# Attention with a threshold and a two-layer network: the first loads through one queue, the first row maximum ahead of a low part, the first x loaded earlier, and three instructions on the row sums on GpSimd

## The chip, the core and the metric

The kernel runs on one core of a Trainium2 chip. The metric is the time of one execution in microseconds on the device, the median of several runs. TensorE (PE) multiplies matrices, VectorE (DVE), ScalarE (ACT) and GpSimd (POOL) work on rows of 128 partitions, and SyncE (SP) issues most transfers. Each engine takes its instructions in the order of its own queue and waits for others by semaphores.

## The reference

```python
scores = (1 / sqrt(64)) * q @ k.T          # batch 8, heads 8, 576 x 576 each, head_dim 64
thresh = max(scores, row) - tau            # tau = 0.02
scores = where(scores >= thresh, scores, -1e9)
attn = exp(scores - max(scores, row))
attn = attn / (sum(attn, row) + 1e-9)
x = (attn @ v)                             # heads side by side: 4608 rows x 512
h = x @ w_in                               # 512 x 2048, float64 weights
g = maximum(h, 0) + alpha * minimum(h, 0)
out = g @ w_out                            # 2048 x 512
```

Only the few scores of a row that lie within tau of the row's maximum count. The products are made as sums of three products of a high part and a low part of each operand.

## The kernel before, in words

The 64 heads are taken as 32 pairs (class Pair), and each pair in nine units: four blocks of 128 queries for each of the two heads, and one unit "t" for the remaining 64 queries of both. The main loop runs over cycles, one for each unit. In cycle i TensorE makes the scores of unit i + 2 (`scores`, tile s: the high part of k, then the low part) and transposes the masked rows of unit i (`turn`, tile t); VectorE takes the row maximum (`rowmax`, nmx, L456) and later masks and sums (`mask`, L476: p times the comparison with thr, and the row's sum into sm); ScalarE makes the exponentials and the threshold (`expo`, L464 and L469). A score tile has two buffers, so the scores of one unit wait for the mask of the unit two before.

Everything else is put into cycles by tables: PREP (loads and the splitting of the next pair's q and k), AVW and AVS (products with v), FINW and FINS (the end of a pair: `recip`, `rturn`, `rout`, `fin_add`, `fin_mul`, `fin_out`). Within a cycle the functions are called in the order in which the tables were entered. The order on TensorE, ScalarE, VectorE and GpSimd is the order of these calls; only the queue of SyncE is ordered by a scheduler.

Pairs 0 to 4 are the whole pairs (WHOLE = 5): their masked rows are not split into high and low parts. While they run, the float64 weights of the first layer's seven chunks are decoded (class Split64) in steps on all three vector engines: `size` on ScalarE, `clamp`, `shift`, `sign` and `power` on VectorE (L143, L146, L151, L156), `rest` and `join` on GpSimd (L77; wri and wti or wro and wto are the temporaries, wi and wo the weights). GpSimd also makes the low part of the next pair's k (kl) and q (qt).

At the end of a pair `recip` makes rv = 1 / (sm + 1e-9) from nine columns of sums; for whole pairs sm + 1e-9 is first multiplied with min(sm + 1e-9, 1). TensorE turns rv (`rturn`), ScalarE copies it (`rout`), it goes to DRAM (rvd) and comes back spread over partitions (rb), and GpSimd multiplies x with it (`fin_mul`). x goes to DRAM (xs).

Pair 0 has its own loading: `load_first` issues two halves for each of two heads, q on ScalarE's queue and k on SyncE's; `prep_first` makes the high part of q (ScalarE, L359), its low part (VectorE, L360), the high part of k (L361) and its low part (L362) for one head.

Once 256 rows of x are complete, the first layer's work on them begins (class Mlp): a cycle loads them (`load_x`, tile xr, from cycle 49 on), XO0 cycles later GpSimd splits them in four parts (`split_part`, L214 and L215), and then TensorE makes one chunk of the hidden layer (tile pha, L226) in every cycle that has room. After the last pair the rest of the network runs alone.

## Time and profile before

| | before |
|---|---|
| median of 3 runs | 1360.91 us (1358.39 to 1362.42) |
| the profiled execution | 1360.37 us |
| its span, first to last instruction | 1358.6 us |
| TensorE busy | 1324.9 us (98%) |
| VectorE busy | 973.6 us (72%) |
| ScalarE busy | 842.4 us (62%) |
| GpSimd busy | 970.8 us (71%) |
| HBM read and written | 105 GB/s over the span |

The busy times are of the whole span; what a stage waits for is seen only in that stage. The lines of the profile name a line of the kernel, the engine, the operation, and the tile that is written and those that are read.

### The profile page before, as it was taken

What the parts mean: (1) busy time and instruction counts of PE and PEld (TensorE: products, weight loads), DVE (VectorE), ACT (ScalarE), POOL (GpSimd) and SP (SyncE); (2) the same over time, 40 slices, a digit from 0 to 9 for tenths busy, and PEclk for the clock granted to TensorE, in tenths of its full rate; (3) what the DMA queues carried; (4) which work ended last, traced back from release to release, by engine and by line L of the source; (5) the groups of instructions that cost most, each with busy time, mean ns of one, the idle gap of its engine ahead of it and who ended that gap; (6) DMA issues with size and microseconds to landing.
All of it is one profiled execution on the core that took longest, in us unless ns stands there. A gap on an engine that the chain in (4) does not pass through costs nothing.

```text
span 1358.6 us, 24051 instructions
## 1 busy us (share of the span) xinstructions
PE 1324.9 (98%) x8041; PEld 1162.3 (86%) x8041; DVE 973.6 (72%) x1843; ACT 842.4 (62%) x1910; POOL 970.8 (71%) x1369
## 2 busy tenths in 40 slices
PE   6988999999999999999999999999999999999999
PEld 4655799999999999999999999988888888888887
DVE  6989889889888888888888874665565744333332
ACT  7888888888888888888888873433332321211110
POOL 3766899899889898988988985775665754433431
PEclk9999999999999999999999999999999999999999
DMA  8653544644544645545445414345555443343222
GB/s 241 183 160 104 152 131 121 166 128 120 160 134 124 165 127 142 140 132 144 141 136 146 117 51 127 109 132 170 183 164 196 134 145 124 109 152 113 93 78 86
DMA packets 113595, 186.04 MB, mean 137 GB/s; under 512 B 16608, under 2 KB 47872, under 8 KB 113472
## 3 DMA queue, kind: packets, MB, share of 16 engines
q1 hardware_dynamic: 113152, 183.92, 46.2%
q8 instruction: 64, 1.05, 0.3%
q10 hardware_dynamic: 320, 0.59, 0.2%
q14 instruction: 59, 0.48, 0.1%
HBM read 104.41 MB, written 37.90 MB: 105 GB/s over the span
## 4 chain that ended last, share of the span: by engine, by line
PE 83%; DVE 6%; ACT 6%; POOL 1%; DMA 1%; issue 1%; ACTq 0%; SPq 0%; POOLq 0%; DVEq 0%
PE acca L256 12%; PE pha L226 12%; PE s L441 10%; PE phc L226 9%; PE av L620 8%; PE accc L256 8%; PE accb L256 7%; PE phb L226 7%; PE t L485 7%; DVE p L476 2%; DVE nmx L456 2%; PE tk L501 1%; PE accc L981 1%; ACT p L464 1%; ACT xh L205 1%
## 5 line engine op out<-in xcount | busy, mean ns | idle before, releaser
L456 DVE TENSOR_REDUCE nmx<-s 128x1 f32<-128x576 f32 x288 | 217.2, 754 | 67.8 <-PE s L441 65.3
L256 PE MATMUL acca<-wo,ga 128*128 128x512 f32 x756 | 224.1, 415 | 0.9 <-ACT xb L631 0.9
L476 DVE SCALAR_TENSOR_TENSOR p<-s,thr,p 128x576 f32<-128x576 f32 x256 | 206.6, 807 | 4.5 <-ACT thr L469 4.4
L464 ACT ACTIVATE p<-s,nmx 128x576 f32<-128x576 f32 x256 | 189.8, 741 | 8.7 <-DVE nmx L456 8.4
L441 PE MATMUL s<-kh,qst 128*128 128x288 f32 x640 | 141.6, 311 | 27.9 <-DVE p L476 16.2
L250 POOL TENSOR_TENSOR gc<-ptc,gc 128x512 fp32r<-128x512 f32 x45 | 58.1, 1292 | 144.0 <-ACT gc L247 144.0
L226 PE MATMUL pha<-xh,wi 128*128 128x256 f32 x784 | 157.9, 285 | 0.2 <-ACT pra L239 0.2
L485 PE MATMUL t<-ident,p 128*128 128x128 f32 x1024 | 154.5, 273 | 0.0
L247 ACT ACTIVATE gc<-ptc 128x512 fp32r<-128x512 f32 x45 | 28.4, 632 | 196.8 <-DVE ptc L951 196.8
L256 PEld LDWEIGHTS acca<-wo,ga 128*128 128x128 f32 x756 | 133.5, 190 | 19.1 <-ACT xb L631 1.4
L441 PEld LDWEIGHTS s<-kh,qst 128*128 128x128 f32 x640 | 100.1, 191 | 54.6 <-issue 26.4
L226 PEld LDWEIGHTS pha<-xh,wi 128*128 128x128 f32 x784 | 128.0, 190 | 6.5 <-ACT pra L239 3.6
L441 PE MATMUL s<-kl,qst 128*128 128x288 f32 x640 | 133.1, 298 | 0.0
L485 PEld LDWEIGHTS t<-ident,p 128*128 128x128 f32 x1024 | 124.4, 141 | 1.3 <-DVE e L551 1.0
L942 POOL TENSOR_TENSOR homexl<-homexr,homexh 128x512 fp32r<-128x512 f32 (+1 forms) x84 | 103.2, 1247 | 22.1 <-ACT homexh L941 22.0
L226 PE MATMUL phc<-homexh,wi 128*128 128x512 f32 x360 | 112.5, 389 | 0.0
L226 PE MATMUL pha<-xl,wi 128*128 128x256 f32 x392 | 110.7, 283 | 0.0
L578 POOL TENSOR_TENSOR rt<-kw,rt 64x128 fp32r<-64x128 f32 x216 | 97.8, 453 | 17.3
L256 PE MATMUL accc<-wo,gc 128*128 128x512 f32 x480 | 110.1, 389 | 0.0
L250 POOL TENSOR_TENSOR ga<-pta,ga 128x256 fp32r<-128x256 f32 x126 | 96.0, 763 | 18.5 <-ACT ga L247 10.1
L256 PEld LDWEIGHTS accc<-wo,gc 128*128 128x128 f32 x480 | 90.1, 188 | 18.7
L551 DVE TENSOR_TENSOR eo<-t,eo 128x512 fp32r<-128x512 f32 (+1 forms) x162 | 94.7, 598 | 12.7 <-ACT eo L547 11.5
(160 smaller groups left out, 3345.2 us busy)
## 6 DMA issues: line engine op xcount, KB each, us to landing
kr<-in_k_dram SPq DMA_DIRECT2D x31, 320.0 KB
rb<-rvd SPq DMA_DIRECT2D x64, 144.0 KB
xs<-xa SPq DMA_DIRECT2D x32, 288.0 KB
pinb<-part SPq DMA_DIRECT2D x36, 256.0 KB
part<-obb SPq DMA_DIRECT2D x36, 256.0 KB
pinc<-part SPq DMA_DIRECT2D x36, 256.0 KB
out_dram<-obc SPq DMA_DIRECT2D x35, 256.0 KB
qr<-in_q_dram SPq DMA_DIRECT2D x31, 288.0 KB
```

The costliest lines, as they stand in the source:

```text
L226: nc.tensor.matmul(ph[:, :n], w[:, c, :], xx[:, c, :n], start=(c == 0 and ti == 0), stop=(c == NCC - 1 and ti == 2),)
L250: nc.gpsimd.tensor_tensor(g[:, 1, :n], t[:, :n], f(g[:, 0, :n]), op=ALU.subtract)
L256: nc.tensor.matmul(acc[:m, :], gg[:, g, o : o + m], w, start=(first and ti == 0), stop=(last and ti == 2))
L441: nc.tensor.matmul(ps[:, h, :288], w, kk[:, a + h * 288 : a + (h + 1) * 288], start=(ki == 0 and i == 0), stop=(ki == 1 and i == n - 1),)
L456: nc.vector.tensor_reduce(self.nmx[:, j : j + 1], self.S[u][0][:, :, :288], axis=AX.XY, op=ALU.max, negate=True)
L464: nc.scalar.activation(pj, ps[:, :, :288], AF.Exp, bias=nmx[:, j : j + 1], scale=1.0)
L476: nc.vector.scalar_tensor_tensor(pj, ps[:, :, :288], thr[:, j : j + 1], pj, op0=ALU.is_ge, op1=ALU.mult, accum_out=self.sm[:, c : c + 1])
L485: nc.tensor.transpose(tb[:, c, :], pt[:, j, j * D + c * P : j * D + (c + 1) * P], ident)
L551: nc.vector.tensor_tensor(dst[1], ps, f(dst[0]), op=ALU.subtract)
L578: nc.gpsimd.tensor_tensor(lo, r, f(hi), op=ALU.subtract)
L620: nc.tensor.matmul(pa[:m, :n], w, x, start=(part == 0 and c == 0), stop=c == NKC)
L942: self.low.tensor_tensor(xl[:, c, :n], xr[:, c, :n], f(xh[:, c, :n]), op=ALU.subtract)
```

## The change

Five things are done together. The eight first transfers all go through SyncE's queue, q ahead of k for each head, and ScalarE's first instruction is the Exp that loads its table. On VectorE the first row maximum stands ahead of the low part of the second head's k, and the negative tau behind it. For whole pairs the sums' addition, minimum and product are three GpSimd instructions, with a new tile ru; VectorE keeps the reciprocal. The first x is split one cycle after its load in place of two, so that layer 1 begins one cycle earlier. Pair 4 has its own table FINL: its reciprocal is turned and sent later, and the load of the first x stands ahead of it.

```diff
+FINL = (9, 12, 14, 14, 18, 19)
-XO, XO0 = 1, 2
+XO, XO0 = 1, 1
...
-            for eng, r, src, e in ((nc.scalar, qr, q, 0), (nc.sync, self.kr, k, D)):
-                for j in range(2):
-                    w = S + j * e
+            for j in range(2):
+                for r, src, w in ((qr, q, S), (self.kr, k, S + j * D)):
                     for half in range(2):
-                        eng.dma_start(
+                        nc.sync.dma_start(
...
             nc.scalar.activation(self.kh[:, c], self.kr[:, c], AF.Copy)
+            if j == 0:
+                self.prep_first_kl(c)
+
+        def prep_first_kl(self, c):
             nc.vector.tensor_tensor(self.kl[:, c], self.kr[:, c], f(self.kh[:, c]), op=ALU.subtract)
...
-            nc.vector.tensor_scalar(self.rv, self.sm, 1e-9, None, op0=ALU.add)
             if self.whole:
-                nc.vector.scalar_tensor_tensor(self.rv, self.rv, 1.0, self.rv, op0=ALU.min, op1=ALU.mult)
+                ru = ap1.tile([P, 9], F32, tag="ru", name=f"ru{self.pi}", bufs=1)
+                nc.gpsimd.tensor_scalar(ru, self.sm, 1e-9, 1.0, op0=ALU.add, op1=ALU.min)
+                nc.gpsimd.tensor_scalar(self.rv, self.sm, 1e-9, None, op0=ALU.add)
+                nc.gpsimd.tensor_tensor(self.rv, self.rv, ru, op=ALU.mult)
+            else:
+                nc.vector.tensor_scalar(self.rv, self.sm, 1e-9, None, op0=ALU.add)
             nc.vector.reciprocal(self.rv, self.rv)
...
-        fin = FINW if p.whole else FINS
+        fin = (FINW, FINL)[p.pi == WHOLE - 1] if p.whole else FINS
...
+        nc.scalar.activation(ntau_sb, ident[:, :1], AF.Exp)
         p.load("k")
-        nc.scalar.activation(ntau_sb, ident[:, :1], AF.Exp)
...
-        nc.vector.tensor_scalar(ntau_sb, tau_sb, -1.0, None, op0=ALU.mult)
         p.load("v")
         for i in range(-3, total + TAIL):
             if i == -1:
+                do(0, "rowmax")
+                p.prep_first_kl(slice(S, KW))
+                nc.vector.tensor_scalar(ntau_sb, tau_sb, -1.0, None, op0=ALU.mult)
+                do(0, "expo")
...
-            else:
+            elif i > 0:
                 do(i + 1, "rowmax")
                 do(i + 1, "expo")
```

The start, on VectorE before: the low parts of q and k of both heads, the negative tau, and then the row maxima of the first two units.

```order
L360 SCALAR_TENSOR_TENSOR qst0_111<-qr0_175,qst0_111 64x576
L362 TENSOR_TENSOR kl0_194<-kr0_174,kh0_193 128x640
L1152 TENSOR_SCALAR ntau_sb_66<-tau_sb_65 128x1
L456 TENSOR_REDUCE nmx0_0_219<-s0_0_209 128x1
L456 TENSOR_REDUCE nmx0_0_219<-s0_1_214 128x1
L476 SCALAR_TENSOR_TENSOR p0_0_222,sm0_208<-s0_0_209,thr0_0_220,p0_0_222 128x576
```

The same place now, with the line numbers of the changed kernel:

```order
L360 SCALAR_TENSOR_TENSOR qst0_111<-qr0_176,qst0_111 64x576
L460 TENSOR_REDUCE nmx0_0_212<-s0_0_207 128x1
L366 TENSOR_TENSOR kl0_194<-kr0_175,kh0_193 128x640
L1165 TENSOR_SCALAR ntau_sb_66<-tau_sb_65 128x1
L460 TENSOR_REDUCE nmx0_0_212<-s0_1_220 128x1
L480 SCALAR_TENSOR_TENSOR p0_0_217,sm0_206<-s0_0_207,thr0_0_213,p0_0_217 128x576
```

The row maximum of unit 0 moved ahead of the low part of the second head's k.

The end of pair 4, on VectorE before (rv4 is made from the sums sm4; wto6 is a weight being decoded, s5_1 and s5_2 are scores of pair 5):

```order
L456 TENSOR_REDUCE nmx5_0_1603<-s5_1_1610 128x1
L636 TENSOR_SCALAR rv4_1656<-sm4_1285 128x9
L638 SCALAR_TENSOR_TENSOR rv4_1656<-rv4_1656 128x9
L639 RECIPROCAL rv4_1656<-rv4_1656 128x9
L151 SCALAR_TENSOR_TENSOR wto6_1566<-wro6_1482,wto6_1566 128x512
L456 TENSOR_REDUCE nmx5_2_1666<-s5_2_1638 128x1
```

VectorE keeps only the reciprocal there (L647 now); the instructions that it waits for stand on GpSimd now as follows, between the joining of the weight wo5 and the low part of pair 6's q:

```order
L78 TENSOR_TENSOR wro5_1354<-wro5_1354 128x256 x2
L78 TENSOR_TENSOR wto5_1460<-wto5_1460,wo5_1572 128x256 x2
L78 TENSOR_TENSOR wo5_1572<-wto5_1460,wro5_1354 128x256 x2
L642 TENSOR_SCALAR ru4_1665<-sm4_1291 128x9
L643 TENSOR_SCALAR rv4_1664<-sm4_1291 128x9
L644 TENSOR_TENSOR rv4_1664<-rv4_1664,ru4_1665 128x9
L407 TENSOR_TENSOR qt6_1698<-qr6_1634,qst0_111 128x576
```

At pairs 0 and 1 the three stand between wti and wi of a weight, at pair 2 between wi and the next wro, and at pair 3, as here, between wo and qt.

The first x, on TensorE before (pha0_0 is the first chunk of layer 1, s6_1 a unit of scores of pair 6):

```order
L691 MATMUL filler2_1905<-ident_60 128x128 x3
L441 MATMUL s6_1_1929<-kh6_1594,qst0_111 128x288 x2
L441 MATMUL s6_1_1929<-kl6_1596,qst0_111 128x288 x2
L485 MATMUL t5_8_1935<-ident_60,p5_3_1853 128x128 x4
L501 MATMUL tk5_3_1940<-ident_60,p5_3_1853 128x128
L226 MATMUL pha0_0_1949<-xh256_0_1802,wi0_358 128x256
```

Now the chunk's matmuls follow the filler at once, and s6_1 stands behind the twelve of them:

```order
L699 MATMUL filler2_1919<-ident_60 128x128 x3
L227 MATMUL pha0_0_1929<-xh256_0_1806,wi0_358 128x256
L227 MATMUL pha0_0_1929<-xl256_0_1807,wi0_358 128x256
L227 MATMUL pha0_0_1929<-xh256_0_1806,wi0_358 128x256 x2
L227 MATMUL pha0_0_1929<-xl256_0_1807,wi0_358 128x256
```

Layer 1's chunks and the sums of layer 2 on the first 256 rows each stand one cycle earlier from here until pair 9.

## Rows read from the trace of the kernel before

**Rows 1.** Busy time by stage: the stretch and its length in us, then for each engine the busy us and the number of instructions, the granted clock of TensorE, the share of the DMA engines, and GB/s.

```profile
0.00:30.00 30.00, 16.86 (x81) 14.06 (x82) 19.30 (x36) 20.63 (x42) 9.54 (x29) 0.94 0.94 272
30.00:140.00 110.00, 100.24 (x538) 65.42 (x536) 98.99 (x192) 95.31 (x209) 75.13 (x96) 1.00 0.53 147
140.00:200.00 60.00, 55.85 (x400) 49.94 (x399) 51.78 (x108) 51.03 (x122) 52.79 (x89) 1.00 0.51 137
200.00:800.00 600.00, 596.65 (x4342) 563.70 (x4341) 525.19 (x1094) 521.31 (x1247) 537.52 (x894) 1.00 0.49 134
```

**Rows 2.** Waits of TensorE from 30 to 140 us: who waited for whom, us in total, times, the longest.

```profile
PE s L441 <- DVE p L476: 9.3, 11, 2.3
```

**Rows 3.** Timeline of the start: start us, duration us, engine, line, operation, tiles, and in brackets the idle time before and who ended it.

```profile
0.73 2.49 ACTq L347 DMA_DIRECT2D qr<-in_q_dram  x4
...
0.74 2.76 SPq L347 DMA_DIRECT2D kr<-in_k_dram  x4
...
5.24 0.68 ACT L359 ACTIVATE qst<-qr 128x576 fp32r<-128x576 f32 x1 [0.49 <-DMA qr<-in_q_dram]
...
8.38 0.68 ACT L359 ACTIVATE qst<-qr 128x576 fp32r<-128x576 f32 x1 [1.28 <-DMA qr<-in_q_dram]
...
8.97 0.72 ACT L361 ACTIVATE kh<-kr 128x640 fp32r<-128x640 f32 x1
...
11.65 0.76 DVE L456 TENSOR_REDUCE nmx<-s 128x1 f32<-128x576 f32 x1 [0.22 <-PE s L441]
```

**Rows 4.** What the DMA engines moved from 0 to 20 us, in 40 slices of 0.5 us.

```profile
GB/s 0 0 0 0 235 295 281 244 181 209 260 216 235 218 167 225 346 364 378 387 406 357 375 363 358 344 346 352 342 352 354 359 363 389 410 360 360 354 366 361
```

**Rows 5.** The chain of waits from 30 to 180 us, some of its pieces: start us, us, what.

```profile
36.70 0.36 DVE rv L636
...
37.99 0.97 DVE wti L151
...
61.60 0.32 DVE rv L636
...
62.79 0.79 DVE wti L146
...
87.25 0.54 DVE rv L638
...
88.64 0.74 DVE nmx L456
...
112.10 0.47 DVE rv L636
...
114.22 1.51 DVE wto L143
...
137.65 0.36 DVE rv L636
...
138.94 0.97 DVE wto L151
...
172.35 1.49 PE pha L226 x12
```

**Rows 6.** Timeline of GpSimd at the ends of the whole pairs (columns as in Rows 3; x2 are two halves).

```profile
36.30 1.42 POOL L77 TENSOR_TENSOR wti<-wti,wi 128x256 f32<-128x256 f32 x2
...
60.47 1.41 POOL L77 TENSOR_TENSOR wti<-wti,wi 128x256 f32<-128x256 f32 x2
...
85.19 1.42 POOL L77 TENSOR_TENSOR wi<-wti,wri 128x256 fp32r<-128x256 f32 x2
...
90.01 2.01 POOL L77 TENSOR_TENSOR qt<-qr,qst 128x288 fp32r<-128x288 f32 x2 [0.70 <-ACT qr L393]
...
112.47 1.43 POOL L77 TENSOR_TENSOR wo<-wto,wro 128x256 fp32r<-128x256 f32 x2
113.87 1.58 POOL L403 TENSOR_TENSOR qt<-qr,qst 128x576 fp32r<-128x576 f32 x1
...
138.62 1.87 POOL L77 TENSOR_TENSOR wo<-wto,wro 128x256 fp32r<-128x256 f32 x2
140.65 1.41 POOL L403 TENSOR_TENSOR qt<-qr,qst 128x576 fp32r<-128x576 f32 x1 [0.15 <-ACT qr L393]
```

**Rows 7.** GpSimd's groups of instructions by line and shape: busy us and mean ns of one, idle us before.

```profile
L578 POOL TENSOR_TENSOR rt<-kw,rt 64x128 fp32r<-64x128 f32 x216 | 97.8, 453 | 17.3
...
L663 POOL TENSOR_SCALAR vs<-xa 64x1 f32<-64x1 f32 x54 | 11.1, 206 | 4.7
...
L108 POOL MEMSET eps_sb<- 128x1 f32 x1 | 0.1, 95 | 0.0
```

**Rows 8.** Timeline of VectorE, one row (columns as in Rows 3).

```profile
90.65 0.71 DVE L151 SCALAR_TENSOR_TENSOR wto<-wro,wto 128x512 int32<-128x512 int32 x1
```

**Rows 9.** TensorE's idle times in its timeline, and two windows with the granted clock (columns as in Rows 3 and Rows 1).

```profile
23.29 0.58 PE L441 MATMUL s<-kh,qst 128*128 128x288 f32 x2 [1.94 <-DVE p_t L476]
...
116.61 0.50 PE L441 MATMUL s<-kh,qst 128*128 128x288 f32 x2 [2.33 <-DVE p L476]
...
24.00:27.00 3.00, 3.00 (x16) 2.95 (x16) 2.43 (x6) 1.85 (x6) 2.83 (x5) 0.50 1.08 265
110.00:120.00 10.00, 7.50 (x41) 4.73 (x40) 9.93 (x18) 7.54 (x17) 9.73 (x13) 1.00 0.75 202
```

**Rows 10.** TensorE's timeline ahead of s6_1 (columns as in Rows 3).

```profile
159.27 0.51 PE L441 MATMUL s<-kh,qst 128*128 128x288 f32 x2 [0.68 <-PE filler L691]
```

## The prediction

> **What bounds the kernel now.** I read the busy time by stage first [rows 1]. From 200 us on TensorE is busy 596.65 of 600 us: nothing but TensorE's own work counts there, and the change gives it the same matmuls. A gain or a loss must therefore come before about 200 us, where TensorE stands idle for 13.1 us (start), 9.8 us (30 to 140) and 4.2 us (140 to 200). The list of waits says for whom: between 30 and 140 us it waits 9.3 us, in 11 pieces, for the masks p of VectorE [rows 2]. The chain of waits comes third. In the stage of the whole pairs 0 to 4 it runs over VectorE, and at the end of every pair over the two instructions on the small sums (rv, L636 and L638) that the change moves [rows 5]. So a microsecond more or less on VectorE there arrives at the end. The timeline of the start comes fourth [rows 3]: the first real work waits for the DMAs of q and k.
>
> **The start.** Before, q goes out on ScalarE's queue and k on SyncE's, four issues each, 0.62 and 0.69 us apiece [rows 3]. ScalarE takes up the second head's q at 8.38, as its last half lands, and its k right behind at 8.97; the second row maximum starts at 11.65, that is 2.68 us after the k. That maximum sets the first masks. All eight transfers hold 1184 KB. Between 2 and 8 us the engines moved 1383 KB, 230 GB/s on average, but part of it was weights and pair 1's data, issued behind k [rows 4]. In one queue those stand behind all eight. At 230 GB/s the 1212 KB (decimal) need 5.3 us from 2.0 on: 7.3, with a little for the completion 7.5. Eight issues at 0.69 end at 6.3, so the issue is not the limit. VectorE has time for the first row maximum (0.76) before the second head's low k, since head 0 also lands earlier. The second maximum then starts at 7.5 + 2.68 = 10.2, a gain of 1.45. Bounds: if the last issue (6.3) needs the 3.3 us that q's second half took from its issue (1.98) to its use (5.24), k lands at 9.5 and the start loses 0.5; if head 0's work alone decides, everything can be 2.0 earlier. I take -1.45, nearest to the measured rate. The weights and pair 1's k go out later; they are first used behind the first exponentials, and I cost that at nothing; if pair 1's k were late, ScalarE would stand still in front of its rounding with the next exponentials queued behind.
>
> The Trainium skill, "DMA: Bandwidth & Descriptors", section "Issuing engines are not separate DMA queues", says that transfers of several issuing engines share the same DMA engines and that using several saves only the issue time. By that rule the move to one queue could at most cost its four issues, and the sum would not change as long as the issues end before the data, as they do in the sum above; no run here shows it yet.
>
> **The small sums of pairs 0 to 4.** VectorE loses L636 and L638 and keeps the reciprocal, which now waits for three GpSimd instructions. What is queued on VectorE behind that wait is decode work and then the next row maximum and mask, for which TensorE waits. GpSimd works in order, so the sums start when the instruction ahead of them in its queue ends. GpSimd has no 128x9 instruction in the trace; the nearest is 0.206 us on 64x1 (L663), with 0.095 (a fill of one column) and 0.453 (64x128) as the outer rows [rows 7]. Three at 0.2 and some 0.05 of hand-over each make 0.75 us; the bounds are 0.44 and 1.5. Now pair by pair, in the times of before [rows 5, 6]:
> Pair 0: GpSimd's wti ends at 37.72, the sums at 38.47, the reciprocal at 38.7. Behind it stands wti of L151. It takes 0.97 in the chain and 0.71 elsewhere [rows 5, 8]; if, as I read the difference, it waits for the GpSimd instruction that has begun, it now waits for the first half (0.71) of the next two and ends at 39.8 in place of 38.96, +0.8. Left alone it would end at 39.3, +0.3.
> Pair 1: wti ends at 61.88, sums 62.63, reciprocal 62.87; L146 behind it ends when the next half does, 63.7 in place of 63.58: +0.1.
> Pair 2: wi ends at 86.61, which is early; sums 87.36, reciprocal 87.6, L146 behind half a wro at 88.3. The next row maximum starts at 88.2 in place of 88.64: -0.4.
> Pair 3: two instructions of wo stand ahead; they end at 113.90, sums 114.65, reciprocal 114.9. By then GpSimd has begun qt (1.58) and is in it until 116.2. In the trace L143 ends at 115.73, 0.28 behind that same qt, and takes 1.51 for it; so I let L156 end 0.3 behind qt, at 116.5, and L143 at 116.85 in place of 115.73: +1.1. Without the hold nothing is lost or gained.
> Pair 4: wo again stands ahead. It took 1.87 with L151 in between, 1.43 in the same shape at pair 3; alone it ends at 140.05. Sums 140.8, reciprocal 141.0; qt (1.41) runs from 140.8 to 142.2; L151 ends at 142.85 in place of 139.91: +2.9. Without the hold +1.75.
> Together 0.8 + 0.1 - 0.4 + 1.1 + 2.9 = +4.5. The two removed instructions (about 1 us at each pair in rows 5) are in this already, because it compares the ends of what follows. Without any hold and with sums of 0.44 it comes to about +0.25; with sums of 1.5, 0.75 more at every pair, to +8.2. I take the middle, since the rows of GpSimd ahead of the sums are measured and only the holds and the small instructions are not.
>
> On this hold the rows and a rule can be weighed. At 90.65 a wto of L151 took 0.71 though GpSimd was in its two qt instructions from 90.01 to 92.02 [rows 6, 8]; L151 at 138.94 took 0.97 and L143 at 114.22 took 1.51 [rows 5]. The Trainium skill, "SBUF — State Buffer", section "Who interferes with whom", says that VectorE with two SBUF inputs and GpSimd lock each other out for a whole instruction, whichever began first. By that rule the price at pair 4 is +2.9; by the row at 90.65 alone it would be +1.75, and the sum of all five pairs about 2.6 lower. The trace has both. In the sum I go by the 1.51, since at pairs 3 and 4 one long qt follows, as there.
>
> **The first x.** Its load leaves the place behind the reciprocals' round trip (rb waits for rvd) and its four splits go one cycle up on GpSimd. Layer 1's first chunk then stands ahead of s6_1 on TensorE, in the cycle in which TensorE stood idle 0.68 us ahead of that s6_1 [rows 10]. Its twelve matmuls (1.49 us in the chain at 172.35 [rows 5]) fill that hole, and later there is as much less to do: -0.6. Bounds: -1.5 if all of it falls into holes up to 200 us, +0.6 if s6_1 passes its lateness on to VectorE. The later reciprocal of pair 4 costs nothing: its x belongs to the second batch and is read cycles later.
>
> **Sum.** -1.45 + 4.5 - 0.6 = +2.45 us. The profiled execution took 1360.37 us (span 1358.6), so 1362.8; it lay 0.5 under the median of the runs, 1360.91. That is +0.14%, and 0.3% (about what a measurement of this kernel can tell from no change) is 4.1 us: no change that can be told.
>
> **Rivals.**
> A. The sums cost no wait. If GpSimd came to them in time, VectorE would save the rv rows of the chain, some 1 us at each of five pairs, 5.2: -1.45 - 5.2 - 0.6 = -7.25, 1353.1. For it: GpSimd is busy only 75 of 110 us in this stage [rows 1]. Against it: at the place of the sums it works without a gap in every pair [rows 6].
> B. The clock falls: slower. After 1.94 us of idle ahead of 23.29 TensorE's granted clock was 0.50 (1.2 of 2.4 GHz) from 24 to 27 us [rows 9]. At pair 3 TensorE would stand 3.4 us for the mask (2.33 now [rows 9], 1.1 more), at pair 4 the 2.9 added and what it waits now. Three microseconds at half the clock are 1.5 lost. One fall gives 1364.3, two 1365.8, and slower counts from 1365.0; so it decides from two falls on, or one with slower sums. Against it: after the 2.33 us ahead of 116.61 the clock stayed at 2.4 GHz, as the window from 110 to 120 shows.
> C. One queue is slower than two: k lands at 9.5, the start loses 0.5, the total is +4.4, 1364.8.
>
> **How the numbers follow.** The sum as it stands 0.55, A 0.08, B 0.20, C 0.17. Of the sum's own case some 3% go below 1356.8 (no hold at all) and 12% over 1365.0 (slow sums); B is slower with 0.6, C with 0.4. Faster: 0.08 + 0.02 = 0.10; slower: 0.07 + 0.12 + 0.07 = 0.26; same 0.64. The bounds of the terms added give 1357.3 to 1369; the case A and the far end of slow sums are left out: 1357.5 to 1366.5.
>
> **What would show it.** In the profile after: the second row maximum of pair 0 near 10.2 and the round of the second head's k near 7.5 (start); VectorE waiting for GpSimd ahead of each reciprocal, most at pairs 3 and 4, and L151 and L156 lengthened behind it (sums); GpSimd rows of some 0.2 us on 128x9; TensorE's wait for the mask behind pair 4's reciprocal near 4 us; granted clock 1.00 there, or 0.50 if B; the wait ahead of s6_1 gone (x). The prediction is wrong if the reciprocals of pairs 3 and 4 start without a wait, or if the k of the second head lands no earlier.

## The result, and the profile after

The changed kernel takes 1369.10 us (median of 4 runs, 1368.89 to 1373.61), the kernel before 1360.54 beside it: a ratio of 1.0071, 95% interval 1.0046 to 1.0097. It is slower, by 8.6 us where +1.9 was forecast, and outside the range, which ended at 1366.5. Two executions far from all others (1870.80 us in f1 below, 3815.49 us of the kernel before beside h1) are left out of the medians in this document.

By stage, for the changed kernel (columns as in Rows 1, with which it is to be compared):

```profile
0.00:30.00 30.00, 17.65 (x84) 14.28 (x84) 20.23 (x38) 21.36 (x42) 9.51 (x29) 0.94 0.92 262
30.00:140.00 110.00, 96.88 (x508) 62.56 (x506) 88.63 (x174) 91.54 (x201) 72.46 (x102) 0.98 0.51 140
140.00:200.00 60.00, 53.44 (x365) 46.29 (x365) 48.65 (x100) 45.75 (x109) 49.38 (x87) 0.97 0.49 128
200.00:600.00 400.00, 397.05 (x2893) 375.20 (x2892) 348.98 (x732) 347.64 (x833) 359.36 (x594) 1.00 0.52 140
600.00:800.00 200.00, 199.24 (x1457) 188.80 (x1456) 177.10 (x368) 173.86 (x417) 179.17 (x299) 1.00 0.48 130
```

TensorE is as full as before from 200 us on (596.29 of 600), so the loss lies ahead of that, as the prediction said of any loss. Between 30 and 200 us two numbers are new. TensorE got through 873 matmuls where it was 938 [rows 1], and the granted clock is no longer 1.00. The waits of TensorE between 30 and 140 us, in the form of Rows 2 (what waits, for whom, us in total, times, longest):

```profile
PE s L445 <- DVE p L480: 9.9, 11, 3.4
PE s L445 <- DMA qst<-qt: 2.7, 1, 2.7
```

The wait for the masks has hardly grown here (pair 4's, 4.02 us, falls behind 140 us). The second line is new: TensorE waits for a DMA, the copy of pair 1's low q from its place on the upper partitions to the lower ones.

Where each microsecond goes is best read by lining the two kernels up. VectorE makes the same row maxima in the same order in both, so the start of the n-th row maximum can be compared in all kernels of this study. The table gives, in us, how much later it starts than in the profile of the kernel before (each number is a difference of two starts in VectorE's timelines; the labels are those of the experiments below):

| row maximum, its start before | changed | e1 | e2 | e3 | e4 | f1 | f2 | g1 | g2 |
|---|---|---|---|---|---|---|---|---|---|
| pair 0, 21.67 | -0.38 | -0.22 | 1.34 | -0.50 | -0.97 | 0.99 | 0.91 | -0.15 | -0.49 |
| ahead of pair 1, 30.20 | -0.55 | -0.78 | 0.79 | -0.49 | -0.96 | 0.43 | 0.91 | -0.71 | -0.49 |
| ahead of pair 0's sums, 35.95 | 3.24 | 1.30 | 0.35 | 2.02 | -0.11 | -0.01 | 0.91 | 1.36 | -0.49 |
| behind them, in pair 1, 44.33 | 3.84 | 1.64 | 2.68 | 2.27 | 0.31 | 0.74 | 0.89 | 1.52 | -0.31 |
| ahead of pair 3's sums, 110.02 | 3.72 | 1.34 | 2.58 | 2.19 | -0.30 | 0.59 | 0.57 | 1.70 | -0.74 |
| behind them, 117.68 | 4.81 | 1.31 | 3.63 | 3.56 | -0.68 | 1.64 | 0.53 | 1.44 | -1.99 |
| ahead of pair 4's sums, 136.90 | 4.79 | 1.32 | 4.86 | 5.56 | -0.69 | 2.90 | 0.51 | 1.44 | -1.99 |
| behind them, 139.83 | 7.79 | 1.32 | 7.86 | 8.57 | 0.25 | 5.90 | 0.51 | 1.43 | -3.25 |
| 148.00 | 9.36 | 1.32 | 9.34 | 8.51 | 1.83 | 8.41 | 0.50 | 1.45 | -1.90 |
| s6_1, 160.78 | 9.78 | 1.77 | 9.78 | 8.95 | 2.28 | 8.43 | 0.93 | 1.45 | -1.94 |
| behind s6_1, 164.09 | 9.14 | 1.12 | 9.14 | 8.31 | 1.64 | 8.43 | 0.29 | 1.44 | -1.97 |
| 182.27 | 10.70 | 2.70 | 10.74 | 9.91 | 3.75 | 8.43 | 1.81 | 1.45 | -1.96 |
| 241.03 | 9.39 | 1.45 | 9.49 | 8.67 | 2.51 | 8.42 | 0.52 | 1.46 | -2.00 |

In the column of the changed kernel four steps stand out: -0.4 to -0.6 at the start, +4.4 as pair 1 begins, +1.1 at pair 3's sums, +4.6 at pair 4's, in two parts (3.0 and then 1.6). From 148 to 241 us, where the first x acts, the number goes up and down by as much as 1.5 and ends where it was. Small steps early in a column mean little: the kernel before, f1, f2 and g2 have the same loads and the same order on VectorE up to pair 0's sums, and yet their profiles lie between -0.49 and +0.99 at 21.67.

**The start.** Rows of SyncE, ScalarE and VectorE in the changed kernel (columns as in Rows 3):

```profile
0.72 1.21 SPq L347 DMA_DIRECT2D qr<-in_q_dram  x2
...
4.53 1.23 SPq L347 DMA_DIRECT2D kr<-in_k_dram  x2
...
8.30 0.74 ACT L361 ACTIVATE kh<-kr 128x640 fp32r<-128x640 f32 x1 [0.63 <-DMA kr<-in_k_dram]
...
11.05 0.76 DVE L460 TENSOR_REDUCE nmx<-s 128x1 f32<-128x576 f32 x1 [0.88 <-PE s L445]
```

The second head's k is taken up at 8.30 where it was 8.97 [rows 3], and the second row maximum comes at 11.05 where it was 11.65. And this is what the DMA engines moved from 0 to 20 us, in slices of 0.5 us as in Rows 4:

```profile
GB/s 0 0 0 0 129 249 263 221 212 212 240 232 212 277 180 45 82 213 346 353 389 394 383 294 340 253 331 381 379 377 363 348 348 354 376 382 390 377 366 356
```

From 7.5 to 8.5 us the engines run nearly dry: 45 and 82 GB/s, where the kernel before had 225 and 346 [rows 4]. The eight issues have ended at 5.76, and what is to follow has only just been issued. From 2 to 7 us both kernels moved about as much, 225 GB/s here and 237 before.

**Pair 1.** SyncE's copies for pair 1's q and k, and then the first scores of pair 1 on TensorE:

```profile
20.34 0.38 SPq L129 DMA_DIRECT2D wri<-in_moe_w_in_dram  x1
22.29 0.46 SPq L410 DMA_DIRECT2D qst<-qst  x1
23.89 0.46 SPq L411 DMA_DIRECT2D qst<-qt  x1
25.05 0.46 SPq L388 DMA_DIRECT2D kh<-kh  x1
28.58 0.46 SPq L388 DMA_DIRECT2D kl<-kl  x1
31.38 0.46 SPq L414 DMA_DIRECT2D qst<-qt  x1
...
33.82 0.50 PE L445 MATMUL s<-kh,qst 128*128 128x288 f32 x2 [2.66 <-DMA qst<-qt]
```

The same last two rows in the kernel before:

```profile
27.34 0.65 SPq L410 DMA_DIRECT2D qst<-qt  x1
...
31.50 0.53 PE L441 MATMUL s<-kh,qst 128*128 128x288 f32 x2
```

The last copy is issued 4.0 us later, and what had no wait before now waits 2.66 us. What SyncE itself waits for ahead of the three copies (in the form of Rows 2, from 20 to 36 us):

```profile
SPq L414 <- DMA qst<-qst: 2.3, 1, 2.3
SPq L410 <- DMA wri<-in_moe_w_in_dram: 1.5, 1, 1.5
SPq L411 <- DMA qr<-in_q_dram: 1.1, 1, 1.1
```

The first copy waits for a weight's load (issued at 13.19) and the second for the q of pair 2 (at 13.72). Neither uses these data, and each is the transfer that SyncE issued eight places earlier. The last copy waits for the first one to land. Behind TensorE's wait the clock falls (windows of 1 us, columns as in Rows 1; the column ahead of the last two is the granted clock):

```profile
35.00:36.00 1.00, 1.00 (x4) 0.37 (x4) 1.00 (x2) 0.58 (x1) 1.00 (x3) 0.50 0.65 138
36.00:37.00 1.00, 1.00 (x3) 0.40 (x2) 1.00 (x4) 0.34 (x2) 1.00 (x2) 0.50 0.96 201
37.00:38.00 1.00, 1.00 (x4) 0.46 (x2) 1.00 (x2) 0.00 (x0) 0.79 (x4) 0.55 1.06 222
```

Half the clock (1.2 of 2.4 GHz) for some 3 us: about 1.5 of the 4.4 us, as an estimate.

**The sums.** GpSimd and VectorE at the ends of pairs 3 and 4 in the changed kernel:

```profile
116.20 1.43 POOL L78 TENSOR_TENSOR wo<-wto,wro 128x256 fp32r<-128x256 f32 x2
117.72 0.26 POOL L642 TENSOR_SCALAR ru<-sm 128x9 f32<-128x9 f32 x1
118.04 0.24 POOL L643 TENSOR_SCALAR rv<-sm 128x9 f32<-128x9 f32 x1
118.37 0.21 POOL L644 TENSOR_TENSOR rv<-rv,ru 128x9 f32<-128x9 f32 x1
118.53 1.40 POOL L407 TENSOR_TENSOR qt<-qr,qst 128x576 fp32r<-128x576 f32 x1
...
118.61 0.22 DVE L647 RECIPROCAL rv<-rv 128x9 f32<-128x9 f32 x1 [2.79 <-POOL rv L644]
118.74 1.48 DVE L157 TENSOR_SCALAR wro<-wto 128x512 int32<-128x512 int32 x1
...
145.75 1.40 POOL L407 TENSOR_TENSOR qt<-qr,qst 128x576 fp32r<-128x576 f32 x1
...
145.83 0.22 DVE L647 RECIPROCAL rv<-rv 128x9 f32<-128x9 f32 x1 [3.39 <-POOL rv L644]
145.96 1.74 DVE L152 SCALAR_TENSOR_TENSOR wto<-wro,wto 128x512 int32<-128x512 int32 x1
```

Here the mechanism is as it was predicted, nearly to the tenth: the reciprocals stand waiting behind the decode of a weight, and the instruction behind them is held by the qt that GpSimd has just begun. Compare 1.48 us for L157 here with 0.42 for the same line elsewhere. TensorE then waits 3.39 us at pair 3 and 4.02 us at pair 4:

```profile
121.43 0.51 PE L445 MATMUL s<-kh,qst 128*128 128x288 f32 x2 [3.39 <-DVE p L480]
...
149.25 0.50 PE L445 MATMUL s<-kh,qst 128*128 128x288 f32 x2 [4.02 <-DVE p L480]
```

Behind the second wait the clock falls once more:

```profile
151.00:152.00 1.00, 1.00 (x4) 0.42 (x2) 1.00 (x2) 0.89 (x2) 0.88 (x3) 0.50 0.94 270
152.00:153.00 1.00, 1.00 (x4) 0.63 (x3) 0.09 (x1) 0.78 (x3) 0.84 (x3) 0.50 0.63 219
153.00:154.00 1.00, 1.00 (x6) 1.00 (x6) 0.00 (x0) 0.00 (x0) 1.00 (x3) 0.52 0.02 6
```

At 241 us the changed kernel is 9.4 us behind, at the end of the span 8.3. The 1.1 us between go at 380 to 409 us, where TensorE has no idle time in either profile. The profiles of f1, f2, g1 and g2 come 1.0 to 1.2 us closer to the kernel before there too, those of e1 and f3 do not, so it is nothing of the change; its cause stays open.

### The profile page after: what moved, and what is told of

Read it like the earlier page. It is cut to its first block, busy times and chain, and to the rows that moved or that the text cites. A ratio compares the mean times of both kernels' runs of the same rounds, so it can differ in the third digit from the quotient of the medians.

```text
span 1366.9 us, 24047 instructions
## 1 busy us (share of the span) xinstructions
PE 1327.6 (97%) x8041; PEld 1163.4 (85%) x8041; DVE 969.8 (71%) x1833; ACT 842.0 (62%) x1910; POOL 973.3 (71%) x1384
## 3 DMA queue, kind: packets, MB, share of 16 engines
q8 instruction: 64, 1.05, 0.3%
## 4 chain that ended last, share of the span: by engine, by line
PE 85%; ACT 6%; DVE 4%; POOL 2%; DMA 2%; issue 1%; SPq 0%; POOLq 0%; ACTq 0%; DVEq 0%
PE acca L257 12%; PE pha L227 12%; PE s L445 10%; PE phc L227 9%; PE av L624 9%; PE accc L257 8%; PE t L489 7%; PE accb L257 7%; PE phb L227 7%; DVE p L480 1%; DVE nmx L460 1%; PE tk L505 1%; PE accc L989 1%; ACT p L468 1%; DMA qst<-qst 1%
## 5 line engine op out<-in xcount | busy, mean ns | idle before, releaser
L950 POOL TENSOR_TENSOR homexl<-homexr,homexh 128x512 fp32r<-128x512 f32 (+1 forms) x84 | 102.9, 1243 | 19.6 <-ACT homexh L949 18.7
```

Source lines behind the costliest of these rows:

```text
L950: self.low.tensor_tensor(xl[:, c, :n], xr[:, c, :n], f(xh[:, c, :n]), op=ALU.subtract)
```

## The experiments

e1 to e4 and f3 are edits of the changed kernel, f1, f2, f4, g1, g2 and h1 of the kernel before. Every ratio is to the kernel before, run beside it on the same chip (medians 1359.4 to 1360.3 us). The profile is of one run each and need not be a typical one; where it is far from the median, the text says so.

### e1: the sums back on VectorE

```diff
+            nc.vector.tensor_scalar(self.rv, self.sm, 1e-9, None, op0=ALU.add)
             if self.whole:
-                ru = ap1.tile([P, 9], F32, tag="ru", name=f"ru{self.pi}", bufs=1)
-                nc.gpsimd.tensor_scalar(ru, self.sm, 1e-9, 1.0, op0=ALU.add, op1=ALU.min)
-                nc.gpsimd.tensor_scalar(self.rv, self.sm, 1e-9, None, op0=ALU.add)
-                nc.gpsimd.tensor_tensor(self.rv, self.rv, ru, op=ALU.mult)
-            else:
-                nc.vector.tensor_scalar(self.rv, self.sm, 1e-9, None, op0=ALU.add)
+                nc.vector.scalar_tensor_tensor(self.rv, self.rv, 1.0, self.rv, op0=ALU.min, op1=ALU.mult)
```

> The changed kernel with the two instructions on the sums on VectorE again for the whole pairs; start and first x as changed. Theory (the sums wait behind the weight decode on GpSimd at pairs 3 and 4): the shift of 1.1 us at pair 3 and of 3.0 us at pair 4 goes, and with it the half clock behind pair 4 (1.6 us), so about 5.7 us less than the changed kernel, 1363.4; what is left over the kernel before is the late q of pair 1. Rival (the sums only stand where a wait would be anyway, and the loss is the start's alone): within 1 us of the changed kernel, 1368 to 1370.

Measured 1363.07 us (1360.69 to 1365.95, 10 runs), ratio 1.0022 (1.0012 to 1.0033). That is the theory's number. In the table nothing is lost any more at pairs 3 and 4 (1.34 to 1.32 over both). What is left is the late copy: TensorE waits 3.07 us for it. No fall of the clock followed in that profile, and the runs spread over 5 us.

### e2: q on ScalarE's queue again

```diff
-                for r, src, w in ((qr, q, S), (self.kr, k, S + j * D)):
+                for eng, r, src, w in ((nc.scalar, qr, q, S), (nc.sync, self.kr, k, S + j * D)):
...
-                        nc.sync.dma_start(
+                        eng.dma_start(
...
-        nc.scalar.activation(ntau_sb, ident[:, :1], AF.Exp)
         p.load("k")
+        nc.scalar.activation(ntau_sb, ident[:, :1], AF.Exp)
```

> The changed kernel with the first pair's q on ScalarE's queue again, and the loading of the exponentials' table behind it as before; the row maximum of unit 0 stays ahead of the second head's low k. Theory (eight issues in one queue push all later loads back, so the copies of pair 1's q come late): TensorE's wait of 2.7 us for the copy of q ahead of pair 1's first scores goes, with the half clock behind it, so 3.9 to 4.2 us less than the changed kernel, 1365. Rival (the order in which weights and copies stand on SyncE is the cause, not the front): here both weight loads stand ahead of all copies of pair 1, so the wait stays at 2 us or more and the time within 1 us of 1369.

Measured 1369.40 us, ratio 1.0068: in time the rival's number, in mechanism the theory's. The copy goes out 3.6 us earlier than in the changed kernel and TensorE has no wait for it:

```profile
27.78 0.59 SPq L414 DMA_DIRECT2D qst<-qt  x1
...
31.67 0.54 PE L445 MATMUL s<-kh,qst 128*128 128x288 f32 x2
```

Both weight loads stand ahead of all copies here, so the rival would have had them late. But about as much is lost again in three other places, which the table shows. The start is 1.3 us later than in the kernel before at 21.67 (0.35 at 35.95). Of the 1.3, 0.9 come from the second head's k: it is there by the time of the first row maximum (at 9.95), and its low part now stands behind that, at 10.74 in place of 9.88. Pair 0's sums now wait 2.0 us for GpSimd, which costs 2.3 with the half clock behind it (0.35 to 2.68):

```profile
39.06 0.22 DVE L647 RECIPROCAL rv<-rv 128x9 f32<-128x9 f32 x1 [2.01 <-POOL rv L644]
```

In the changed kernel the same reciprocal starts without a wait, at 39.86, since the late copy has held up VectorE by then. And the clock fell behind pair 3 too (1.2 us more). Undoing one part of a change uncovered a cost of another part.

### e3: fillers in the two waits

```diff
             do(i, "mask")
+            if i in (7, 46):
+                filler.run(9)
             do(i + 2, "scores")
```

> The changed kernel with nine more filler matmuls (2.5 us) on TensorE ahead of pair 1's first scores and ahead of s5_3, the two places where it waits 2.7 and 4.0 us. Theory (the waits themselves cost, and on top the clock that falls behind them): the waits for the copy and for the mask end when they ended, but the granted clock stays at 1.00 behind both, and 1.5 us at each place come back: 1366. Rival (the half clock is hidden in the waits for VectorE that follow): clock 1.00, time unchanged at 1369. Or the clock falls all the same: then it isn't the idle time that does it.

Measured 1369.60 us, ratio 1.0070: no change of the time, which is the rival's number. The windows say why, and it is not the rival's reason. At both filled places the granted clock stays at 1.00, and the table has the gains, 1.6 us in pair 1 (2.27 for 3.84) and 1.6 behind pair 4 (no step from 8.57 to 8.51, where the changed kernel went from 7.79 to 9.36). But now the clock fell behind the unfilled wait of pair 3, where it had not fallen in the changed kernel, and took 2.0 us:

```profile
35.00:36.00 1.00, 1.00 (x5) 0.58 (x5) 1.00 (x2) 0.55 (x1) 1.00 (x3) 1.00 0.67 143
...
151.00:152.00 1.00, 1.00 (x7) 0.50 (x5) 1.00 (x3) 0.69 (x2) 0.28 (x1) 1.00 0.86 199
...
120.00:121.00 1.00, 1.00 (x5) 0.98 (x6) 1.00 (x2) 0.55 (x1) 1.00 (x3) 0.50 1.02 239
```

So the half clock is worth about 1.5 us at each place, and where the idle time was filled it did not come. Whether it comes after a given wait differs between profiles of programs that are alike around it.

### e4: the sums one cycle earlier

```diff
+        if p.whole:
+            first_at_cycle(o + fin[0] - 1, p.sums)
         at_cycle(o + fin[0], p.recip)
```

The three GpSimd instructions are a function of their own here, `sums`; `recip` keeps the reciprocal.

> The changed kernel with the three GpSimd instructions on the sums one cycle earlier, behind the pair's last mask and ahead of that cycle's weight decode; the reciprocal stays where it is. Theory (it is the place in GpSimd's queue, not the engine, that costs): no reciprocal waits for GpSimd, the shifts at pairs 3 and 4 and the half clock go (5.7 us), and VectorE saves its two instructions, up to 1 us at each of the last four pairs: 1360 to 1363.4. Rival (any work on GpSimd there delays the weights by 1 us and VectorE behind them): half of it or less comes back, 1366 or more.

Measured 1366.29 us (1362.65 to 1367.93), ratio 1.0049: half of the 5.7 us came back, which in time is the rival's number. The profile is of the fastest of the four runs, 3.6 us under the median, so where the other runs lose more isn't seen. In it pair 1's copy is issued at 29.48 and TensorE waits only 1.31 us for it. Pair 3 now gains 0.4 us in place of losing 1.1. Pair 4 still loses, 0.9 and then 1.6 of half clock, since the weight's first two products there are called a cycle earlier still, ahead of the sums:

```profile
138.95 0.22 DVE L650 RECIPROCAL rv<-rv 128x9 f32<-128x9 f32 x1 [1.99 <-POOL rv L644]
```

The wait is still there, 2.0 us of the 3.4. The place in GpSimd's queue is what decides, and this place was not early enough; g2 takes that up.

### f1: the sums alone

The first diff of e1 the other way round, in the kernel before.

> The kernel before with nothing changed but the two instructions on the sums, which go to GpSimd as three. Theory (the sums stand behind the weight decode): with no late q in front, pair 0's reciprocal waits about 2 us for GpSimd and costs 1.8 us, pair 3 costs 1.0, pair 4 costs 3.0: +5.8 us, 1365.3 by 1359.5 of before, and 1.5 us more for every fall of the clock behind one of these waits, 1368.3 with two. My own working from the trace of before had 0.8 at pair 0, 4.5 in all and no fall: 1364. Rival (pair 0's sums cost nothing, as it looks in the changed kernel): +4.0, 1363.5.

Measured 1367.83 us (1366.30 to 1368.72, 3 runs), ratio 1.0060 (1.0044 to 1.0075): the theory's number with two falls. The table gives the steps: 0.75 at pair 0 (-0.01 to 0.74), nothing that lasts at pairs 1 and 2, 1.05 and 1.3 of half clock at pair 3, 3.0 and 2.5 of half clock at pair 4. The theory's 1.8 for pair 0 was too large: its reciprocal waits 2.00 us as in e2, but most of that is not passed on. The 0.8 of the prediction was near.

### f2: the first x alone

```diff
+FINL = (9, 12, 14, 14, 18, 19)
-XO, XO0 = 1, 2
+XO, XO0 = 1, 1
...
-        fin = FINW if p.whole else FINS
+        fin = (FINW, FINL)[p.pi == WHOLE - 1] if p.whole else FINS
```

> The kernel before with only the first x one cycle earlier and the later end of pair 4's reciprocals. Theory (layer 1's first chunk fills the hole ahead of s6_1, and the 1.5 us that the changed kernel loses around 182 us, at pair 5's own end, belong to this part): the row maxima stand 0.6 us earlier from 164 us on, 0.9 later from 182 us on, and at the end nothing of it is left within 0.5 us, 1359.0 to 1360.0. Rival (the 0.6 us stay): 1358.9, and row maxima earlier by 0.6 at 250 us.

Measured 1360.01 us (11 runs), ratio 1.0002 (0.9993 to 1.0011): nothing, as the theory had it. Up to the row maximum of s6_1, at 160.78, 0.43 us are lost (0.50 to 0.93), up to the next one 0.64 are gained (to 0.29), at 182 us 1.5 are lost, and by 241 us it is 0.52, where it stood at 139.83. The 0.43 is an instruction of layer 1 (L239) that now stands ahead of that row maximum. The 0.64 is VectorE's first instruction on pair 5's sums, here in the kernel before and then in f2:

```profile
162.78 0.80 DVE L636 TENSOR_SCALAR rv<-sm 128x9 f32<-128x9 f32 x1
...
163.71 0.16 DVE L637 TENSOR_SCALAR rv<-sm 128x9 f32<-128x9 f32 x1
```

In the kernel before it ends 0.04 us behind a GpSimd instruction on kl (161.99 to 163.54); in f2 GpSimd is through with that one at 161.75. The loss is at the end of pair 5. Layer 1's work on GpSimd is a cycle earlier too, and VectorE waits for the product with rb behind it:

```profile
183.54 0.62 DVE L675 TENSOR_SCALAR rb<-rb,vs 128x576 f32<-128x576 f32 x1 [1.30 <-POOL xa L672]
```

The same row in the kernel before has no wait. TensorE, which is nearly full by then, makes up for it within 50 us, and for the gain as well.

### f3 and f4: two queues, q ahead of k on both

f3 is the changed kernel with the sums on VectorE (as e1), the Exp behind the loads (as e2) and this start; f4 is the kernel before with the first x of f2 and the same loads, the low part of the second head's k ahead of the first row maximum as before.

```diff
-                        nc.sync.dma_start(
+                        (nc.sync, nc.scalar)[half].dma_start(
```

> The changed kernel's first x, VectorE's sums as before, and another start: the eight loads in the changed kernel's order (q ahead of k, head 0 ahead of head 1), but one half of each on SyncE's queue and the other on ScalarE's, the table behind them; the first row maximum stays ahead of the second head's low k. Theory (the eight issues in one queue are what makes pair 1's q late): eight issues end near 3.3 us again, the copies of pair 1's q are issued by 27.8 and TensorE doesn't wait for them; the second row maximum comes 0.6 us or more earlier than in the kernel before: 1358 to 1359. Rival (the order of the loads is the cause): a wait of 1.3 to 3 us for the copy as with one queue, 1361 to 1363.

> The same two queues and first x, but VectorE makes the second head's low k ahead of the first row maximum, as the kernel before. Theory (with two queues head 0 lands early enough, so the first row maximum fits ahead of the second head's low k): 0.3 to 0.8 us slower than with the row maximum first, 1359 to 1359.5. Rival (the second head's k lands before VectorE has made the first row maximum, as with q on ScalarE's queue, where the row maximum ahead cost 0.8): faster than with the row maximum first, 1358.

Measured 1360.09 us for f3 (ratio 1.0001, 0.9993 to 1.0010) and 1360.43 for f4 (1.0007, 0.9998 to 1.0015). Neither beats the kernel before, and between the two orders on VectorE these runs don't tell. In both the last copy for pair 1 is issued later than with the loads of before (28.91 and 29.43; 27.34 to 28.71 in the profiles of the kernel before, f1, f2 and g2), and TensorE waits 1.71 and 1.42 us for it. The theory had 27.8 and no wait; the wait is the rival's, the time is not. f3's profile is of the slowest of its 11 runs, with a fall of the clock behind pair 3 that cost 1.0 us. So two queues alone don't bring the copy in time in these profiles when the loads are in this order, and what the start gains ends in front of the copy.

### g1: one queue alone

The two lines of the loads in the change's diff, and nothing else, in the kernel before.

> The kernel before with nothing changed but the first eight loads: all on SyncE's queue, q ahead of k. Theory (eight issues of 0.62 us in one queue let the DMA engines run dry near 8 us and push the copies of pair 1's q back): GB/s falls under 100 near 7.5 us, the last copy of pair 1's q is issued after 29.4 us and TensorE waits 1.3 to 3 us for it, half a clock behind it in some runs: 1361 to 1364, by 1359.4 of before. Rival (it takes the moved row maximum as well, which changes what stands ahead on VectorE and with it SyncE's order): no wait for the copy, 1359 to 1360.

Measured 1363.27 us (1360.68 to 1364.43), ratio 1.0028 (1.0017 to 1.0039). The theory holds: 37 and 86 GB/s at 7.5 and 8.0 us, the copy issued at 30.70, a wait of 2.90. The moved row maximum isn't needed for it. The profile is of the fastest of the seven runs, and its granted clock is 1.00 over the whole span, also behind the wait of 2.90. The six others have 0.996 or 0.997 over the span: a half clock somewhere, which no profile of this kernel shows. The queue alone costs some 3.8 us, the sums alone 8.4, the first x nothing that can be told; the whole change costs 8.6, since two of the losses hide one another in part and the clock doesn't fall everywhere.

### h1: one queue, six issues

```diff
-            for j in range(2):
-                for r, src, w in ((qr, q, S), (self.kr, k, S + j * D)):
-                    for half in range(2):
+            for half in range(2):
+                rows = slice(half * D, (half + 1) * D)
+                nc.sync.dma_start(self.qr[rows], q[0, 0].rearrange("(j d) w -> d j w", j=2))
+            for j in range(2):
+                for half in range(2):
...
```

The diff is to g1; k is loaded in four pieces as there, q in two.

> The kernel before with the first loads all on SyncE's queue, q ahead of k as in the changed kernel, but q of both heads in one DMA for each half: six issues in place of eight. The weights and copies stand on SyncE in the same order as in the changed kernel and in queue_only. Theory (the eight issues make the later loads late): six issues end near 4.5 us, the DMA engines don't run dry near 8 us, the last copy of pair 1's q is issued by 28.7 us, TensorE waits less than 1 us for it: 1359 to 1361 by 1359.5 of before. Rival (the order on SyncE, with the two weight loads among the copies, makes the copy late): the copy is issued after 29.4 us and the wait of 1.3 to 3 us stays: 1362 to 1364.

Measured 1361.03 us beside 1360.3, ratio 1.0010 (0.9999 to 1.0021), less than half of g1's loss. The DMA engines don't run dry any more:

```profile
GB/s 0 0 0 0 92 272 309 235 263 184 254 244 240 241 173 195 332 352 372 377 408 342 390 368 355 356 358 342 352 348 346 352 375 386 400 371 364 347 370 377
```

The copy is issued at 29.68, 1.0 us earlier than in g1, and the wait is 1.69 in place of 2.90. By the times the number of issues is a good part of it, with the order on SyncE as in g1. By the copy alone it is not settled: 29.68 lies within what the profiles with eight issues on one queue have (29.48 in e4 to 31.38). The copy is still 1.0 us later than the latest with the loads of before, and the theory's less than 1 us of wait was not reached.

The order on SyncE sorts the profiles more cleanly. In all six with the loads on one queue (the changed kernel, e1, e3, e4, g1, h1) a weight's load is issued between the copies of pair 1's low k and those of its q, at 19.6 to 20.7, and the last copy then waits 1.9 to 2.4 us for the first one to land. In the seven others the last weight is issued by 17.9, ahead of the copies of low k, and the last copy follows the one before it at once. So the loads are shown to make the copy late; how much of that is the time of the issues and how much the weight among the copies, no run here separates.

### g2: the sums ahead of the weight

f1 and e4 together, with one line more: the two products `rest` of the one weight that stands in the cycle ahead are called a cycle later.

```diff
-        at_cycle(c + 5, w.rest)
+        at_cycle(c + 5 + (c % 9 == 2 and c + 5 < 9 * WHOLE), w.rest)
```

> The kernel before with the two instructions on the sums as three on GpSimd, ahead of the weight decode of the cycle before the reciprocal (the last products of one weight per pair wait one cycle for that). My rival A of the prediction, put to the test: no reciprocal waits for GpSimd, VectorE is quit of two instructions at each of five pairs, up to 1 us each where the chain runs over it (pairs 2 to 4 by the runs so far): 1356.5 to 1358.5 by 1359.4 of before. Rival (GpSimd's three instructions now wait for the pair's last mask and hold up the weight behind them, whose decode VectorE and ScalarE then wait for): no gain or a loss, 1359 to 1363.

Measured 1358.04 us (1357.28 to 1359.20, 11 runs), ratio 0.9990 (0.9981 to 0.9999): faster than both kernels, by 1.4 us, which is less than the runs of either spread (1.9 and 3.2 us). At pair 4 the three instructions are through long before they are wanted:

```profile
134.76 0.21 POOL L640 TENSOR_TENSOR rv<-rv,ru 128x9 f32<-128x9 f32 x1
134.93 1.18 POOL L77 TENSOR_TENSOR wro<-wro 128x256 f32<-128x256 f32 x2
...
135.58 0.20 DVE L646 RECIPROCAL rv<-rv 128x9 f32<-128x9 f32 x1
135.70 0.96 DVE L151 SCALAR_TENSOR_TENSOR wto<-wro,wto 128x512 int32<-128x512 int32 x1
```

The reciprocal follows the row maximum without a wait. Only pair 2's still waits, 0.56 us. From pair 3's sums on the profile is 2.0 us ahead, of which 0.5 was there ahead of pair 0's sums, where nothing had been changed.

## Why the prediction was wrong, step by step

**The start: sized too high, and its cover wrong.** The step was -1.45, from the second head's k at 7.5. It was taken up at 8.30, and the gain was 0.6 at the second row maximum and 0.4 by 22 us, within what profiles with one and the same start differ by. The eight issues ended at 5.76, before the 6.3 worked out. The sentence "so the issue is not the limit" was true for the eight loads and false for what stands behind them. A half of 144 KB takes 0.62 us to issue, and that is about as long as its data need at 230 GB/s; so there was never more than a little in hand, and when the eighth had been issued nothing else was ready. The Trainium skill, "DMA: Bandwidth & Descriptors", section "Issuing engines are not separate DMA queues", says that a second issuing engine saves only the issue time, which is usually small beside the transfer. By the rows here it was not small: 0.62 us beside 0.64 for the data, and 45 GB/s at 7.5 us with one queue, 225 with two. Whether the issue time is all that the second queue saved is not shown.

**The step that failed: what the start pushes back "I cost at nothing".** The prediction said of pair 1's data that they are first used behind the first exponentials, and looked at its k on ScalarE. The user that counts is TensorE, through pair 1's q: split on two engines, copied by SyncE in three steps, each of which waits for a landing. Two of these landings are of transfers that the copies don't use, issued eight places earlier (1.5 and 1.1 us, L410 and L411 in the changed kernel), so lateness in front is handed on. The chain had little in hand: the copy issued at 27.34 before was used at 31.50; e1 and g1, where TensorE stood waiting, used theirs 2.4 us after its issue, which makes an estimate of 1.7 us in hand. It came 4.0 us later. The wait of 2.7 us and the half clock behind it make up +4.4 us, half of the loss; g1 shows that it is the loads. Its size differs from profile to profile: with the same loads the column at 44.33 runs from 0.31 (e4) to 3.84. By which road the loads make the copy late, the time of eight issues or the weight's load that then stands among the copies, stays open (h1). It is not in the range either, whose bounds for the start ended at +0.5. Rival C had the sign right (one queue slower) and the place wrong: the second head's k was not late.

**The small sums: right in place, mechanism and size.** Forecast by pair +0.8, +0.1, -0.4, +1.1 and +2.9; measured in f1, without the falls of the clock, +0.75, 0.0, -0.15, +1.05 and +3.0, together 4.65 for 4.5. (Pair 2's row maximum came 0.3 earlier, but that did not last; and f2, with the sums as before, has -0.3 over the same stretch.) In the changed kernel pairs 3 and 4 give 1.1 and 3.0, and pair 0's share hides behind the late copy. The three instructions take 0.26, 0.24 and 0.21 us, 0.9 with their hand-overs, in place of 0.75. The hold was decided for the long price: L157 ends 0.29 us behind qt, L152 0.55 behind it, where the prediction's ends imply 0.3 and 0.65. By the rule of the Trainium skill ("SBUF — State Buffer", "Who interferes with whom", a lock for a whole instruction) the price at pair 4 was 2.9, by the row at 90.65 alone 1.75; the trace agrees with the rule, at 3.0. Why the row at 90.65 was not held stays open.

**The clock: a rival that came true.** B stood at 0.20 and spoke of pairs 3 and 4. The clock fell behind pair 4 (1.6 us) and, which was not named, behind pair 1 (1.5 us). It did not fall behind pair 3's 3.39 us in the changed kernel; it did in f1, e2 and e3. Against it I had put one wait of 2.33 us that was not followed by a fall [rows 9]. One case was too few to argue from, and one price for all falls too: they cost 1.0 to 2.5 us here.

**The first x: its number met by luck.** TensorE's wait ahead of s6_1 went, as forecast, but behind the chunk s6_1's scores start later (160.40 in f2, 159.27 before), and its row maximum came 0.43 later, not 0.6 earlier. The 0.64 gained up to the row maximum after it is VectorE's, an instruction on the sums that GpSimd no longer holds (f2), and not the filled hole. Net of both it is 0.2 at 164.09. And the row at which GpSimd's moved work is waited for (pair 5's product) was not looked at, and from 200 us on a full TensorE levels such things out: f2 measures nothing.

**The sum.** +2.45 was forecast. With the start at -0.5, the copy at 4.4, the sums at 4.0 (their pairs 1 to 4 as they show in the changed kernel), the second fall at 1.6 and the first x at nothing, it is +9.5, and the table has 9.4 at 241 us. The bounds of the prediction's terms are added up wrongly there: on 1360.37 they give 1357.1 and 1369.7, not 1357.3 and 1369. The measured 1369.10 lies inside them and outside the stated range, but by a term that they do not hold. Rival A had a gain of 5.2 for the sums. There is a gain, but it needs another place in GpSimd's queue, and g2, which has that place, shows 1.4 by the medians.

## What to carry to other kernels

When a change moves the issue of early transfers, follow every later transfer on that queue to the engine that uses its data, and write down how much it has in hand; a start that gains 0.6 us is worth nothing if the next stage's data come 4 us later. Look also at what the scheduler then puts between the transfers. Work that goes to an engine "with time to spare" costs what stands ahead of it in that engine's queue at that moment: the same three instructions cost 4 us and more behind a weight's decode, and gained 1.4 us ahead of it. And a wait of TensorE of the lengths seen here (1.94 to 4.05 us) may be paid twice, once as idle time and once as half the clock behind it, so both belong into the price.

## What was not expected of the hardware

The granted clock fell to 0.50 behind idle times of 2.66 us (pair 1), 4.02 (pair 4) and, in e4, about 2 us, and did not fall behind 3.39 us at pair 3 of the changed kernel, where e3, with a wait as long at the same place, has 0.50. Nor did it fall behind 3.07 and 2.90 us at pair 1 in e1 and g1, while behind pair 3's usual wait it fell in f3 and h1 (2.21 and 2.03 us) and not in the kernel before (2.33). Near 23 us, on the other hand, it went with the length: all eight profiles with a wait of 1.94 or 1.95 us there show the fall, and the five with 0.82 to 1.20 us there show none. The length of the idle time alone did not decide it in these rows. And transfers of 144 KB to 64 partitions took as long to issue on one queue as their data took to move: 0.62 us each, and 0.64 at 230 GB/s. The queue kept up with the data, but had nothing in hand, and a gap of 1 us at 45 to 82 GB/s came behind the last.
